# Leaving out the filler products at the front of a retention and feed-forward kernel

## The chip, the cores and the metric

The kernel runs on one core of a Trainium2 chip, as one launch. The metric is the device time of that launch in microseconds (us). Three timed runs of the kernel before gave 626.86, 627.22 and 627.27 us; the median is 627.22 us.

## The reference

Three stages follow each other. The first is a retention with a decay for each head, over 2 batches, 8 heads, 768 positions and 64 elements of a head:

```
for t in range(S):
    state = gamma * state + outer(k[:, :, t], v[:, :, t])
    y[:, :, t] = scale * (q[:, :, t] @ state)          # scale = 1/sqrt(64)
x = y as 1536 rows of 512
g = softplus(x @ w_in);  x = g @ w_out                  # 512 -> 2048 -> 512
xn = x / sqrt(mean(x*x) + 1e-6) * rms_g
out = (silu(xn @ w_gate) * (xn @ w_val)) @ w_out2       # 512 -> 1536 -> 512
```

The weights of the two feed-forward stages arrive as 64-bit floats. They are converted on the chip into a high and a low part, and each of their products is computed as three products of parts.

## The kernel before, in words

**Tiles and stages.** The 1536 rows are 12 chunks of 128 (6 for each batch), and 3 blocks of 512. For each chunk the retention is computed in its chunked form: `step_t` transposes q and k of a chunk on TensorE (`turn`, line 261) and moves them out, q by VectorE (line 263, multiplied by a table of decays) and k by ScalarE (line 268). `step_s` multiplies the two (line 280; two heads at a time, in two PSUM banks), and VectorE multiplies the result by a mask (line 282, one instruction for each bank). `step_y` adds the product with the running state (line 316, not in a batch's first chunk) to the product of the masked scores with v (line 323). `step_u` makes the new state (line 293). Ahead of that, GpSimd multiplies v by decays in `prep` (line 250).

**Order of the work.** Every engine works its instructions off in the order in which the code writes them. The program opens with chunk 0: `keep_busy(6)`, the table of decays (`wide` on VectorE, then `table` with four transposes, line 237), the masks, `step_t(0, 1, (0, 1))`, two more `keep_busy` products, `step_s(0)` and `step_t(1)`. The loop over the first four chunks then runs, for each g, `step_y(g)`, `step_u(g)`, `step_s(g + 1)` and `step_t(g + 2)`. From chunk 4 on, products of the first feed-forward layer (line 340, 512 columns each) stand between the steps of the chunks; after chunk 11 TensorE has feed-forward products alone.

**The fillers.** `keep_busy(n)` takes one PSUM bank and writes n products of a 128 by 128 tile of ones with itself to it (line 214). Nobody reads them. There are ten: six ahead of the table's transposes, one each ahead of the transposes of q and of k of chunk 0, and two ahead of the scores of chunk 0.

**Loads.** q, k and v come by DMA in rows of 64 floats. The queues of SyncE and ScalarE share the halves of q and k of chunk 0; everything after that is issued by SyncE in the order of the code. q, k and v of all chunks share ten buffers (`s2_p`), so the load of v of chunk 2 waits until q of chunk 0 has been transposed.

**Banks.** `bank()` hands out the eight PSUM banks: four from a pool that goes round, and up to four accumulator banks that are lent in between, by a count of the calls (`banks["n"]`). Each `keep_busy` is one such call.

Of the kernel before, what the change touches and what calls it, by code (L numbers as in the profile page):

```python
# [15 lines left out]
P = 128  # L16
# [10 lines left out]
def retention_softplus_swiglu(ctx: ExitStack, tc: tile.TileContext, q, k, v, w_in, w_out,  # L27
                              w_gate, w_val, w_out2, rms_g, decay, out):
    nc = tc.nc
# [30 lines left out]
    def bank(name):  # L60
        n, s = banks["n"], len(banks["spare"])
        banks["n"] += 1
        if (n + 1) * s // (4 + s) > n * s // (4 + s):
            banks["spare"].append(banks["spare"].pop(0))
            return acc_bank(banks["spare"][-1])
        return ps.tile([P, N], F32, tag="ps", name=name)

    def acc_bank(m):
        return pa.tile([P, N], F32, tag=f"acc{m}", name=f"acc{m}")
# [30 lines left out]
    def load_next(g, weight=False):  # L100
        if g + 1 < NCH:
            load(g + 1, 0)
            load(g + 1, 1)
        if weight:
            load_weight()
        if g < NCH:
            load(g, 2)


    ones = const.tile([P, P], F32)  # L110
# [15 lines left out]
    order = []  # L126
# [81 lines left out]
            load_weight()  # L208


    def keep_busy(n):
        t = bank("busy")
        for _ in range(n):
            nc.tensor.matmul(t[:, 0:P], lhsT=ones, rhs=ones, start=True, stop=True)


    x, tr, tp = {}, {}, {}


# [7 lines left out]
    def pair(t, j):  # L227
        return t[:, 2 * j:2 * j + 2, :].rearrange("p h d -> p (h d)")

    def wide():  # L230
        nc.vector.tensor_copy(tab[:, 1].rearrange("p j (e d) -> p j e d", e=2),
                              dec[:, 0, 1, :].rearrange("p (e j) -> p j e", e=2)[:, :, :, None].to_broadcast([P, NP, 2, D]))
# [7 lines left out]
    def masks():  # L240
        nc.vector.scalar_tensor_tensor(out=back, in0=dec[:, 1, 1], scalar=float(D) ** 0.5, in1=dec[:, 0, 0],
                                       op0=ALU.mult, op1=ALU.mult)
        for e in range(2):
            nc.vector.tensor_tensor(out=mask[e], in0=causal[:, None, :].to_broadcast([P, NP, P]),
                                    in1=back.rearrange("p (e j) -> p e j", e=2)[:, e, :, None].to_broadcast([P, NP, P]),
                                    op=ALU.mult)

    def prep(g):
        t = qkv[g][2]
        nc.gpsimd.tensor_tensor(out=t, in0=t, in1=dec[:, 1, 0, :, None].to_broadcast([P, H, D]), op=ALU.mult)  # L250

    def turn(g, busy, order):
        t = at_p.tile([P, 4, NP, P], F32, tag="at", name="at")
        tr[g] = t
        tp[g] = []
        for i in order:
            if busy:
                keep_busy(busy)
            pt = bank("pt").rearrange("p (j t) -> p j t", j=NP)
            for j in range(NP):  # L260
                nc.tensor.transpose(pt[:, j, :], pair(qkv[g][i], j), ident)  # L261
            tp[g].append(pt)
        nc.vector.tensor_tensor(out=t[:, 0], in0=tp[g][order.index(0)], in1=tab[:, 0], op=ALU.mult)
        if g == NCH - 1:
            free.append(WS - 1)

    def turned(g, order):
        nc.scalar.activation(out=tr[g][:, 1], in_=tp.pop(g)[order.index(1)], func=AF.Copy)

    def step_t(g, busy=0, order=(1, 0)):  # L270
        turn(g, busy, order)
        turned(g, order)

    def step_s(g):
        t = tr[g]
        sc = [bank("sc").rearrange("p (j t) -> p j t", j=NP) for _ in range(2)]
        for j in range(NP):
            for e in range(2):
                r = slice(e * D, (e + 1) * D)
                nc.tensor.matmul(sc[e][:, j, :], lhsT=t[r, 1, j, :], rhs=t[r, 0, j, :], start=True, stop=True)  # L280
        for e in range(2):
            nc.vector.tensor_tensor(out=t[:, 2 + e], in0=sc[e], in1=mask[e], op=ALU.mult)
# [252 lines left out]
                step()  # L535

    rg = const.tile([P, KC], F32)
    keep_busy(6)
    wide()
    table()  # L540
    masks()
    step_t(0, 1, (0, 1))
    load_next(1)
    load_weight()
    prep(0)
    keep_busy(2)
    step_s(0)
    step_t(1)
    nc.scalar.activation(out=step, in_=tab[:, 0, :, 0], func=AF.Copy, scale=float(D) ** 0.5)
    for g in range(CB):  # L550
        load_next(g + 2)
        if g:
            load_weight()
        prep(g + 1)
        if g == CB - 1:
            nc.sync.dma_start(out=rg, in_=rms_g.rearrange("(k p) -> p k", p=P))
        step_y(g)
        step_u(g)
        step_s(g + 1)
        flush(False)  # L560
        if g < CB - 1:
            step_t(g + 2)
        flush(False)
        if 0 < g < CB - 1:
            convert()

    pend = None
    for gr in range(NG1):
        for b in range(NB):
# [6 lines left out]
            if gr == 0 and b < NB - 1:  # L576
                for o in range(G1):
                    g = (b + 1) * CB + o
# [27 lines left out]
    for gr in range(NG2):  # L606
        for b in range(NB):
# [8 lines left out]
            n = 0  # L616
# [56 lines left out]
```

## Time and profile before

| | |
|---|---|
| median of the timed runs | 627.22 us (626.86 to 627.27) |
| span of the profiled execution, first to last instruction | 3531.3 us |
| time of the profiled execution around its span | not recorded |
| TensorE busy in it | 3526.4 us (100%), 3308 products |
| VectorE, ScalarE, GpSimd busy | 360.4, 325.9, 187.2 us |
| granted TensorE clock recorded | 1.000 throughout |
| HBM read, written | 45.14 MB, 3.15 MB |

How to read it: the profiled execution took more than five times as long as the timed ones. Its times on TensorE are therefore not those of a timed run, and each reading of it has to say how it is carried over. The page's busy time of an engine counts the stretches in which it works at something; a wait row tells how long an engine stood idle and what ended that.

### The profile page before, as it was taken

To read this page: it belongs to the slowest core of one execution; us is meant where nothing else is said; L and a number is where in the kernel's file an instruction comes from. 1 tells how busy PE (TensorE), PEld (TensorE's weight loads), DVE (VectorE), ACT (ScalarE), POOL (GpSimd) and SP (SyncE) were. 2 spreads that over 40 slices of the span, in tenths; PEclk is the share of its full clock that TensorE was granted. 3 is DMA by queue.
4 is the path that set the end of the run, shared out by engine and by line. 5 is a ranking of instruction groups with operands and counts; after the bars stand their busy time and mean duration, and the time that the engine had idled before them with its cause. 6 is when DMAs were issued, how large, how long until landed. Compare 5 with 4: busy or idle time off the path is not lost.

```text
span 3531.3 us, 8590 instructions
## 1 busy us (share of the span) xinstructions
PE 3526.4 (100%) x3308; PEld 2460.6 (70%) x3308; DVE 360.4 (10%) x613; ACT 325.9 (9%) x555; POOL 187.2 (5%) x156
## 2 busy tenths in 40 slices
PE   9999999999999999999999999999999999999999
PEld 8777666666666666666776766666666666666666
DVE  1111001101101010011111100000110011100000
ACT  0111011111101010011110010000000000000000
POOL 0001000000000000000000000000000000000000
DMA  3110000000000000000000000000000000000000
GB/s 76 45 33 21 6 12 12 18 18 18 12 0 12 18 18 0 6 18 0 6 18 18 6 18 18 0 12 6 18 18 0 12 10 14 0 0 3 9 6 18
DMA packets 65560, 48.84 MB, mean 14 GB/s; under 512 B 39792, under 2 KB 60528, under 8 KB 65520
## 3 DMA queue, kind: packets, MB, share of 16 engines
q1 hardware_dynamic: 64320, 47.90, 4.6%
q8 instruction: 26, 0.43, 0.0%
q10 hardware_dynamic: 1200, 0.39, 0.0%
q14 instruction: 14, 0.11, 0.0%
HBM read 45.14 MB, written 3.15 MB: 14 GB/s over the span
## 4 chain that ended last, share of the span: by engine, by line
PE 100%; DVE 0%; ACT 0%; issue 0%
PE h L340 19%; PE h_w_val L340 14%; PE h_w_gate L340 14%; PE l L376 12%; PE l L494 10%; PE acc L376 9%; PE acc L494 6%; PE acc L340 6%; PE sc L280 1%; PE y L323 1%; PE pt L261 1%; PE acc L261 1%; PE acc L323 1%; PE acc L280 1%; PE acc L293 1%; PE y L316 0%
## 5 line engine op out<-in xcount | busy, mean ns | idle before, releaser
L340 PE MATMUL h<-x,ws_w_in 128*128 128x512 f32 x516 | 699.5, 1697 | 0.0
L340 PEld LDWEIGHTS h<-x,ws_w_in 128*128 128x128 f32 x516 | 469.4, 911 | 209.0 <-issue 209.0
L340 PE MATMUL h_w_val<-xn,ws_w_val 128*128 128x512 f32 x384 | 519.5, 1693 | 0.0
L340 PE MATMUL h_w_gate<-xn,ws_w_gate 128*128 128x512 f32 x372 | 502.9, 1694 | 0.0
L340 PEld LDWEIGHTS h_w_val<-xn,ws_w_val 128*128 128x128 f32 x384 | 351.1, 916 | 156.0 <-issue 156.0
L340 PEld LDWEIGHTS h_w_gate<-xn,ws_w_gate 128*128 128x128 f32 x372 | 340.1, 914 | 151.8 <-issue 151.4
L376 PE MATMUL l<-g,ws_w_out 128*128 128x512 f32 x324 | 438.4, 1691 | 0.0
L376 PEld LDWEIGHTS l<-g,ws_w_out 128*128 128x128 f32 x324 | 295.3, 912 | 131.7 <-issue 129.2
L494 PE MATMUL l<-ws_w_out,g 128*128 128x512 f32 x261 | 354.6, 1697 | 0.0
L376 PE MATMUL acc<-g,ws_w_out 128*128 128x512 f32 x252 | 340.6, 1699 | 0.0
L494 PEld LDWEIGHTS l<-ws_w_out,g 128*128 128x128 f32 x261 | 236.7, 908 | 106.0 <-issue 104.4
L376 PEld LDWEIGHTS acc<-g,ws_w_out 128*128 128x128 f32 x252 | 229.5, 914 | 102.6 <-issue 100.5
L494 PE MATMUL acc<-ws_w_out,g 128*128 128x512 f32 x171 | 231.1, 1696 | 0.0
L494 PEld LDWEIGHTS acc<-ws_w_out,g 128*128 128x128 f32 x171 | 156.4, 915 | 69.9 <-issue 69.1
L171 POOL TENSOR_TENSOR c<-w,c 128x512 uint32<-128x512 uint32 x68 | 86.0, 1264 | 1635.3 <-DVE w L169 1279.8
L360 DVE SCALAR_TENSOR_TENSOR t<-h,t 128x512 f32<-128x512 f32 x43 | 29.7, 692 | 990.7 <-ACT t L359 990.7
L122 ACT ACTIVATE g<-t 128x512 fp32r<-128x512 f32 x84 | 52.9, 630 | 720.5 <-DVE t L475 686.2
L357 ACT ACTIVATE t<-h 128x512 f32<-128x512 f32 x43 | 25.7, 597 | 1002.7 <-PE h L340 1002.7
L471 ACT ACTIVATE t<-t 128x512 f32<-128x512 f32 x36 | 22.7, 630 | 701.1 <-DVE t L470 701.1
L340 PE MATMUL acc<-x,ws_w_in 128*128 128x512 f32 x60 | 82.6, 1715 | 0.0
L340 PE MATMUL acc<-xn,ws_w_gate 128*128 128x512 f32 x60 | 81.9, 1701 | 0.0
L475 DVE TENSOR_TENSOR t<-h_w_val,t 128x512 f32<-128x512 f32 x32 | 22.1, 691 | 559.3 <-PE h_w_val L340 559.3
(128 smaller groups left out, 1579.8 us busy)
## 6 DMA issues: line engine op xcount, KB each, us to landing
st_w_out<-in_moe_w_out_dram SPq DMA_DIRECT2D x28, 512.0 KB, 3.2
st_w_in<-in_moe_w_in_dram SPq DMA_DIRECT2D x16, 512.0 KB, 3.8
st_w_gate<-in_moe_w_gate_dram SPq DMA_DIRECT2D x12, 512.0 KB, 3.5
st_w_val<-in_moe_w_val_dram SPq DMA_DIRECT2D x12, 512.0 KB, 3.5
v<-in_v_dram SPq DMA_DIRECT2D x12, 256.0 KB, 3.8
q<-in_q_dram SPq DMA_DIRECT2D x23, 128.0 KB, 3.5
k<-in_k_dram SPq DMA_DIRECT2D x23, 128.0 KB, 2.6
out_dram<-o SPq DMA_DIRECT2D x11, 256.0 KB, 2.0
```

Source lines behind the costliest of these rows:

```text
L122: nc.scalar.activation(out=hi, in_=src, func=AF.Copy)
L171: nc.gpsimd.tensor_tensor(out=c, in0=w, in1=c, op=ALU.add)
L261: nc.tensor.transpose(pt[:, j, :], pair(qkv[g][i], j), ident)
L280: nc.tensor.matmul(sc[e][:, j, :], lhsT=t[r, 1, j, :], rhs=t[r, 0, j, :], start=True, stop=True)
L293: nc.tensor.matmul(u[e * D:(e + 1) * D, j, :], lhsT=kk[:, h, :], rhs=vv[:, NP * e + j, :], start=True, stop=True, skip_group_check=True)
L323: nc.tensor.matmul(ys[e][h * D:(h + 1) * D, i, :], lhsT=qkv[g][2][:, NP * e + j, :], rhs=t[:, 2 + e, j, :], start=(c == 0 and i == 0), sto ...
L340: nc.tensor.matmul(h, lhsT=w[:, i, kk * P:(kk + 1) * P], rhs=src[:, j, kk, :], start=(n == 0), stop=(n == 3 * KC - 1))
L357: nc.scalar.activation(out=t, in_=h, func=AF.Abs)
L360: nc.vector.scalar_tensor_tensor(out=t, in0=h, scalar=0.0, in1=t, op0=ALU.max, op1=ALU.add)
L376: nc.tensor.matmul(p, lhsT=w[:, i, m * P:(m + 1) * P], rhs=g_t[b, f][:, j, :], start=(n == 0 and f == (0 if keep else fs[0])), stop=(n == ...
L471: nc.scalar.activation(out=t, in_=t, func=AF.Silu)
L494: nc.tensor.matmul(p, lhsT=g_t[b, f][:, j, m * P:(m + 1) * P], rhs=w[:, i, :], start=(n == 0 and f == (0 if keep else grp[0])), stop=(n == ...
```

## The change

All four calls of `keep_busy`, ten products in all, are left out, and the function with them; `turn` and `step_t` lose the argument that asked for it.

```
-    def keep_busy(n):
-        t = bank("busy")
-        for _ in range(n):
-            nc.tensor.matmul(t[:, 0:P], lhsT=ones, rhs=ones, start=True, stop=True)
...
-    def turn(g, busy, order):
+    def turn(g, order):
...
         for i in order:
-            if busy:
-                keep_busy(busy)
             pt = bank("pt").rearrange("p (j t) -> p j t", j=NP)
...
-    keep_busy(6)
     wide()
     table()
     masks()
-    step_t(0, 1, (0, 1))
+    step_t(0, order=(0, 1))
     load_next(1)
     load_weight()
     prep(0)
-    keep_busy(2)
     step_s(0)
```

TensorE's order at the program's start, in the kernel before (`busy` are the fillers, `acc0` to `acc3` lent accumulator banks, `ident` the identity of the transposes, `at` the tile of transposed q and k):

```order
L214 MATMUL busy_130<-ones_109 128x128 [waits DVE_49]
L214 MATMUL busy_130<-ones_109 128x128 x5
L237 MATMUL acc0_138<-ident_111,tab_122 128x128 [waits DVE_49,Pool_49]
L237 MATMUL acc0_138<-ident_111,tab_122 128x128 x3
L214 MATMUL busy_148<-ones_109 128x128
L261 MATMUL acc1_150<-ident_111,q0_95 128x128 [waits DMAHW2_49,DMAHW0_49]
L261 MATMUL acc1_150<-ident_111,q0_95 128x128 x3
L214 MATMUL busy_155<-ones_109 128x128
L261 MATMUL acc2_157<-ident_111,k0_98 128x128 [waits DMAHW4_49,DMAHW3_49]
L261 MATMUL acc2_157<-ident_111,k0_98 128x128 x3
L214 MATMUL busy_175<-ones_109 128x128 x2
```

The same place in the changed kernel, up to the first of the scores:

```order
L231 MATMUL pt_131<-ident_111,tab_122 128x128 [waits DVE_49,Pool_49]
L231 MATMUL pt_131<-ident_111,tab_122 128x128 x3
L253 MATMUL acc0_141<-ident_111,q0_95 128x128 [waits DMAHW2_49,DMAHW0_49]
L253 MATMUL acc0_141<-ident_111,q0_95 128x128 x3
L253 MATMUL pt_146<-ident_111,k0_98 128x128 [waits DMAHW4_49,DMAHW3_49]
L253 MATMUL pt_146<-ident_111,k0_98 128x128 x3
L272 MATMUL acc1_164<-at_140 128x128 [waits DVE_49,Activation_49]
```

The table's transposes are now TensorE's first work, and every transpose follows the one before it with nothing between; the banks shift by the four calls that are gone.

Around chunk 11, where the lent banks change from four to two to none, TensorE's order before (transposes of k and q, the first layer's products, the state's product):

```order
L261 MATMUL pt_1082<-ident_111,k11_907 128x128 [waits DMAHW3_49,DMAHW2_49]
L261 MATMUL pt_1082<-ident_111,k11_907 128x128 x3
L261 MATMUL pt_1087<-ident_111,q11_904 128x128 [waits DMAHW1_49,DMAHW0_49,DVE_49]
L261 MATMUL pt_1087<-ident_111,q11_904 128x128 x3
L340 MATMUL acc2_1094<-x1_533,ws_w_in_589 128x512 [waits PE_49]
L340 MATMUL acc2_1094<-x1_533,ws_w_in_589 128x512 x11
L316 MATMUL y_1119<-at_983,state0_119 64x128 [waits DVE_49]
L316 MATMUL y_1120<-at_983,state0_119 64x128 [waits DVE_49,Activation_49]
```

And in the changed kernel:

```order
L253 MATMUL acc2_1068<-ident_111,k11_893 128x128 [waits DMAHW2_49,DMAHW3_49,DVE_49,PE_49]
L253 MATMUL acc2_1068<-ident_111,k11_893 128x128 x3
L253 MATMUL pt_1073<-ident_111,q11_890 128x128 [waits DMAHW1_49,DMAHW0_49]
L253 MATMUL pt_1073<-ident_111,q11_890 128x128 x3
L332 MATMUL h_1080<-x1_519,ws_w_in_575 128x512 x12
L308 MATMUL acc3_1105<-at_969,state0_119 64x128 [waits DVE_49]
L308 MATMUL y_1106<-at_969,state0_119 64x128
```

The same products stand in the same order; two of the bank waits have moved from q's transposes and the first layer to k's transposes.

## Rows read from the trace of the kernel before

**Rows 1.** The page's head and its busy times by engine.

```profile
span 3531.3 us, 8590 instructions
PE 3526.4 (100%) x3308; PEld 2460.6 (70%) x3308; DVE 360.4 (10%) x613; ACT 325.9 (9%) x555; POOL 187.2 (5%) x156
```

**Rows 2.** Timeline of weight loads: start, duration (us), engine, line, operation.

```profile
1513.84 0.88 PEld L340 LDWEIGHTS h<-x,ws_w_in 128*128 128x128 f32 x1 [0.39 <-issue]
1515.12 0.87 PEld L340 LDWEIGHTS h<-x,ws_w_in 128*128 128x128 f32 x1 [0.40 <-issue]
```

**Rows 3.** Stretches: each engine's busy us, then granted clock, DMA share, GB/s.

```profile
0.00:9.30 9.30, 8.18 (x12) 8.04 (x13) 1.96 (x5) 1.28 (x1) 2.18 (x9) 1.00 0.96 180
9.30:22.70 13.40, 13.40 (x21) 11.22 (x19) 0.69 (x1) 1.19 (x2) 2.08 (x2) 1.00 0.66 133
```

**Rows 4.** The chain that ended last, opening stretch: start, us, engine, tile, line.

```profile
1.12 8.54 PE busy L214 x12
9.65 2.56 PE acc L237 x4
13.67 2.56 PE acc L261 x4
17.50 2.73 PE acc L261 x4
20.24 2.56 PE busy L214 x4
36.54 2.56 PE y L323 x4
39.09 2.73 PE acc L293 x8
118.26 15.87 PE acc L340 x12
```

**Rows 5.** Timeline of the opening on VectorE, ScalarE and TensorE.

```profile
2.84 0.43 DVE L231 COPY tab<-dec 128x512 f32<-128x512 f32 x1 [1.77 <-DMA dec<-decay_dram]
20.27 0.60 ACT L268 ACTIVATE at<-acc 128x512 f32<-128x512 f32 x1 [7.43 <-PE acc L261]
22.72 1.31 PE L280 MATMUL acc<-at 64*128 64x128 f32 x1
26.89 0.98 PE L280 MATMUL acc<-at 64*128 64x128 f32 x1
27.53 0.98 PE L280 MATMUL acc<-at 64*128 64x128 f32 x1
28.54 0.69 DVE L282 TENSOR_TENSOR at<-acc,mask 128x512 f32<-128x512 f32 x1 [11.52 <-PE acc L280]
29.15 0.68 DVE L282 TENSOR_TENSOR at<-sc,mask 128x512 f32<-128x512 f32 x1
```

**Rows 6.** Timeline of the opening: loads on SyncE's queue, GpSimd's work on v.

```profile
1.23 0.42 SPq L83 DMA_DIRECT2D q<-in_q_dram  x1
1.70 0.50 SPq L83 DMA_DIRECT2D k<-in_k_dram  x1
8.01 1.04 POOL L250 TENSOR_TENSOR v<-v,dec 128x512 f32<-128x512 f32 x1 [6.13 <-DMA v<-in_v_dram]
11.76 1.09 SPq L83 DMA_DIRECT2D k<-in_k_dram  x1
12.60 1.04 POOL L250 TENSOR_TENSOR v<-v,dec 128x512 f32<-128x512 f32 x1 [3.55 <-DMA v<-in_v_dram]
16.25 0.37 SPq L80 DMA_DIRECT2D v<-in_v_dram  x1
```

**Rows 7.** Loads of three short windows: tile, queue, count, size, us to landing.

```profile
q<-in_q_dram SPq DMA_DIRECT2D x1, 128.0 KB, 3.4
...
k<-in_k_dram SPq DMA_DIRECT2D x1, 128.0 KB, 3.8
...
k<-in_k_dram SPq DMA_DIRECT2D x1, 128.0 KB, 4.6
```

More of the change, by code (lines that the diff above doesn't have):

```diff
@@ L268, in turned, with step_t @@
         nc.scalar.activation(out=tr[g][:, 1], in_=tp.pop(g)[order.index(1)], func=AF.Copy)
-    def step_t(g, busy=0, order=(1, 0)):
-        turn(g, busy, order)
+    def step_t(g, order=(1, 0)):
+        turn(g, order)
         turned(g, order)
```

## The prediction

> **What bounds the kernel now.** I read the page's head first. TensorE is busy for 3526.4 of 3531.3 us [rows 1]: in the profiled execution nothing else bounds. But that span is 5.63 times the median time, 627.22 us, so the second thing to read is TensorE's pace. In the feed-forward part the weight loads of successive 512-column products start 1.28 us apart [rows 2]. By the loops there are 2448 such products (576 and 576 in the first feed-forward stage, 864 and 432 in the second); at this pace they alone take 3133 us. The timed runs cannot have that pace. The stretches show the clock as 1.00, the upper level of 2.4 GHz, even while that pace holds [rows 3], so the clock column does not explain it. The Trainium skill ("TensorE: Matmul & The Clock Gate", the caveat in "Seeing it yourself") says that clock events in a trace have been seen to be unreliable; this trace agrees, with 1.00 beside 1.28 us.
>
> I carry TensorE's rows over by a factor. It is at least 5.63, if a timed run were all TensorE. I take 6: 3526.4 / 6 = 588 us, which leaves 39 us for launch, waits at the front and the end. A sixth stands for the upper clock, a third for the lower level (1.2 GHz). The other engines and the DMA keep their times; I have no reason to scale them.
>
> Then the opening. In the chain of waits the fillers stand in the path with 8.54 us for the first six and more for the others, behind them the table's transposes, those of q and k (2.56 to 2.73 us for each four), and the scores [rows 4]. Each filler is two records on TensorE (12 for six), 20 records of 0.64 us, the distance of the last two score products' starts [rows 5].
>
> Last, the loads. DMA is 96% busy up to 9.3 us [rows 3]. The second half of q of chunk 0 is issued at 1.23 and lands 3.4 later, at 4.6; k's at 1.70 + 3.8 = 5.5; GpSimd starts on v of chunk 0 at 8.01 and of chunk 1 at 12.60, each at its landing; k of chunk 3 lands at 11.76 + 4.6 = 16.4 [rows 6, 7]. These times owe nothing to TensorE.
>
> **The change, part by part.** First against the profiled execution's own time, its span (what lies around it was not recorded). Twenty records go, 20 x 0.64 = 12.8 us. Given back: TensorE then waits from 1.1 to 3.3 us for VectorE's copy of the table, which starts at 2.84 and takes 0.43 [rows 5], 2.2 us; and the two fillers ahead of the scores covered ScalarE's move of k, 0.60 [rows 5], which is now open. 12.8 - 2.2 - 0.6 = 10.0 us. The loads of chunk 1 are in by 12.6, ahead of the scores' end at about 18, so nothing else is late: an execution with this pace would come to 3521 us, 0.3% less.
>
> In a timed run most of that vanishes, because the loads do not shrink with the factor. I write both openings out with TensorE at the lower level until its clock rises (record 0.21, four transposes 0.85, scores 8 x 0.21 = 1.7, `y` 1.7, `u` 0.9).
>
> Before: six fillers 1.1 to 3.7, table to 4.5, filler to 4.95, q to 5.8, filler to 6.2, k to 7.1, two fillers to 7.9. ScalarE has k ready at 7.1 + 0.6 + 0.1 = 7.8. Scores from 7.9. TensorE has had no pause since 1.1, and I choose to take the upper level from here on: scores to 8.75, two masks of 0.69 on VectorE [rows 5] to about 10.2, transposes of chunk 1 meanwhile, `y(0)` to 10.75, `u(0)` to 11.2, scores of chunk 1 to 12.05, their masks to about 13.8 (VectorE also has x and the state to write). v of chunk 1 is ready at 12.60 + 1.04 = 13.64 [rows 6]: `y(1)` is pinned by VectorE and the load alike, and ends at 14.6.
>
> After: table 3.3 to 4.15, q from its landing 4.7 to 5.55, k to 6.45, ScalarE to 7.1, scores from 7.15: 0.75 us earlier. At the lower level they end at 8.85 and the masks at 10.3, as before. Transposes of chunk 1 to 10.55, `y(0)` to 12.25. If the clock has risen by then, `u(0)` ends at 12.7, scores of chunk 1 at 13.55, masks at 15.0, `y(1)` at 15.55, some 0.95 us later than before.
>
> What takes that up is the next load. v of chunk 2 was issued at 16.25 in the profile, behind q's transposes [rows 6]; in a timed run it follows directly on k of chunk 3. At the 133 to 180 GB/s of these stretches [rows 3] its 256 KB take 1.5 to 2.0 us, and behind a landing at 16.4 that is 17.9 to 18.4, plus 1.04 for GpSimd: `y(2)` cannot start before about 19. In both versions TensorE has the scores and transposes for it done by 18.2. So the front meets again at chunk 2, and what is left is the bank shift.
>
> That shift moves two waits around chunk 11, from q's transposes and the first layer to k's transposes. The trace of before does not show a bank wait as TensorE's idle time there. Its bound is one eviction on either side, 0.69 us as for a mask [rows 5], below nothing too; I take 0, for the same work stands behind both.
>
> Sum: -0.75 at the scores, +0.75 from the slower scores, +0.95 by `y(1)` and -0.95 at the load of v, 0 for the banks. I add 0.2 for a late rise of the clock: 627.4 us.
>
> **A rule that speaks against this.** The clock column never leaves 1.00 [rows 3], so no row shows a rise here. The Trainium skill ("TensorE: Matmul & The Clock Gate", "What's actually happening") says that the array starts at the lower clock and that activity releases it. By that rule the fillers buy an early rise, and without them the front could stay at the lower level; that is the first rival.
>
> **The rivals.**
>
> *Slower: the clock stays down through the front.* If the clock rises late in the kernel after, every us past about 12.5 costs half a us, since the work runs at half pace and its slack at the load of v of chunk 2 is used up. Slower than 0.2% (1.25 us) it becomes if the rise comes after 15; at 20 it costs 3.75 us (631.0). The far end is no rise before the first 512-column products: from the scores at 22.72 to 118.26 [rows 4, 5] are 95.5 us, a third of it 31.8, so that these start at 39 instead of about 25.5: +13.5, 641 us. For it: no row shows when the clock rises, and after the change TensorE's work begins 2.2 us later and pauses twice, for q and for ScalarE, before the scores. Against it: from 7.15 on TensorE has no pause in the working above, as before it had none from 1.1 on, and that leaves until 15 for the rise.
>
> *Faster: the fillers are on the path and no load is.* If v of chunks 1 and 2 lands earlier in timed runs, or if the clock is at its upper level from the start, the scores' 0.75 us is kept: 626.5. With an eviction's wait saved too (0.69) it is 1.45, 625.8. Against it: DMA is at 96% there.
>
> *The banks alone decide.* The front meets again, and the shifted waits around chunk 11 add or save up to 0.69: 626.5 to 627.9.
>
> **How the numbers follow.** A measurement of this kernel can tell about 0.2%, 1.25 us, from no change. The forecast, hidden by the loads with 626.9 to 628.2, has 0.48; the slower rival 0.28; the faster one 0.16, of which 0.10 passes 0.2%; the banks 0.08. So faster 0.10, same 0.48 + 0.06 + 0.08 = 0.62, slower 0.28. The range runs from 626.2 (below lies most of the 0.10) to 630.5, a rise at about 19 us, above which I leave 0.11.
>
> **What would show it.** In a profile of the changed kernel at the timed runs' pace, the scores of chunk 0 start near 7.2 us, not 7.9; `y(2)` starts right behind GpSimd's work on v of chunk 2, at about 19 us; the first 512-column product starts at the same time as before within 0.5 us. A TensorE that never waits for v in the front, with a granted clock at the lower level past 15 us, proves the forecast wrong, and so does a time outside 626.0 to 628.5. If that profile has the slow pace again, its span should be near 3521 us.

## The result and the profile after

The changed kernel is slower: 631.97 us as the median of four runs (630.83 to 632.28) against 627.25 (626.86 to 627.72) for the kernel before, timed beside it. The ratio is 1.0072, with a 95% interval of 1.0058 to 1.0087. Forecast were 627.4 us in a range of 626.2 to 630.5, with most of the chance on no change. The time lies outside the range.

The profiled execution that stands ahead of the prediction had TensorE at about a sixth of the pace of every other profile of this study, and the cause was not found; so here the kernel before is read from a second profile, whose span is 625.6 us and whose own time is 627.37 (1.8 us lie around the span). The profile of the changed kernel has a span of 630.5 and a time of 632.28 us. These are the heads of the two, before first; they answer to [rows 1].

```profile
span 625.6 us, 8590 instructions
PE 615.0 (98%) x3308; PEld 510.1 (82%) x3308; DVE 387.5 (62%) x613; ACT 322.1 (51%) x555; POOL 193.3 (31%) x156
```

```profile
span 630.5 us, 8550 instructions
PE 616.4 (98%) x3288; PEld 509.9 (81%) x3288; DVE 385.7 (61%) x613; ACT 322.0 (51%) x555; POOL 193.5 (31%) x156
```

The 20 records of the ten fillers are gone (3308 to 3288), and TensorE's busy time has still grown.

**The front came out as forecast: almost nothing of its difference is left.** The timeline of the kernel before (start, duration, engine, line, operation): scores of chunk 0, the transposes behind them, `y` of chunk 1, the transposes of k of chunk 3, GpSimd's work on v of chunk 2, `y` of chunk 2, and the first product of 512 columns.

```profile
7.83 0.37 PE L280 MATMUL acc<-at 64*128 64x128 f32 x1 [0.24 <-ACT at L268]
8.49 0.27 PE L280 MATMUL acc<-at 64*128 64x128 f32 x1
8.61 0.27 PE L280 MATMUL acc<-at 64*128 64x128 f32 x1
8.93 0.66 PE L261 MATMUL acc<-ident,k 128*128 128x128 f32 x4
14.15 0.66 PE L323 MATMUL y<-at,v 128*64 128x128 f32 x8
17.57 0.63 PE L261 MATMUL acc<-ident,k 128*128 128x128 f32 x4 [0.77 <-DMA k<-in_k_dram]
18.63 1.04 POOL L250 TENSOR_TENSOR v<-v,dec 128x512 f32<-128x512 f32 x1 [5.04 <-DMA v<-in_v_dram]
19.72 0.66 PE L323 MATMUL acc<-at,v 128*64 128x128 f32 x8 [0.49 <-POOL v L250]
27.41 3.00 PE L340 MATMUL acc<-x,ws_w_in 128*128 128x512 f32 x12
```

The same places in the changed kernel (its transposes of k of chunk 3 have no wait and are not shown):

```profile
7.28 0.58 PE L272 MATMUL acc<-at 64*128 64x128 f32 x1 [0.69 <-ACT at L260]
8.50 0.42 PE L272 MATMUL acc<-at 64*128 64x128 f32 x1
8.71 0.42 PE L272 MATMUL acc<-at 64*128 64x128 f32 x1
9.28 1.12 PE L253 MATMUL acc<-ident,k 128*128 128x128 f32 x4
15.69 0.66 PE L315 MATMUL y<-at,v 128*64 128x128 f32 x8
18.56 1.04 POOL L244 TENSOR_TENSOR v<-v,dec 128x512 f32<-128x512 f32 x1 [5.08 <-DMA v<-in_v_dram]
19.89 0.66 PE L315 MATMUL acc<-at,v 128*64 128x128 f32 x8
27.56 2.99 PE L332 MATMUL acc<-x,ws_w_in 128*128 128x512 f32 x12
```

The scores start 0.55 us earlier, and their products follow each other every 0.21 us instead of every 0.12. That is the pace of the lower level of the clock without the fillers, and of the upper one with them: the four transposes behind the scores take 1.12 and 0.66 us, and four transposes further on take 1.09 us where the granted clock stands as 0.50 and 0.66 us where it stands as 1.00 (shown below). In the front itself the granted clock stands as 1.00 in both traces, so the level is read there from the pace alone. At `y` of chunk 1 the changed kernel is 1.54 us behind. Then the loads take nearly all of it up: the kernel before waits 0.77 us for k of chunk 3 and 0.49 us for v of chunk 2, and the changed kernel, coming later, waits for neither. At `y` of chunk 2 0.17 us is left, and at the first 512-column product 0.15 us.

**The loss lies at one place, 71 to 80 us.** A table of stretches of 2 us there (each engine's busy us with its count, then granted clock, DMA share, GB/s), before and after; [rows 3] have the same columns.

```profile
70.00:72.00 2.00, 1.85 (x23) 1.76 (x24) 1.75 (x3) 1.17 (x3) 1.82 (x2) 1.00 0.55 153
72.00:74.00 2.00, 2.00 (x12) 1.68 (x10) 2.00 (x7) 1.60 (x3) 0.89 (x1) 1.00 0.31 109
74.00:76.00 2.00, 2.00 (x29) 1.38 (x29) 1.97 (x7) 1.48 (x4) 0.41 (x1) 1.00 0.00 0
76.00:78.00 2.00, 1.84 (x42) 1.70 (x39) 1.87 (x3) 1.11 (x3) 1.18 (x1) 1.00 0.09 18
```

```profile
70.00:72.00 2.00, 0.91 (x16) 0.72 (x14) 1.75 (x3) 1.18 (x3) 1.42 (x2) 1.00 0.82 227
72.00:74.00 2.00, 0.00 (x0) 0.00 (x0) 2.00 (x8) 1.74 (x3) 1.28 (x1) 0.82 0.10 35
74.00:76.00 2.00, 1.90 (x9) 1.93 (x10) 1.97 (x4) 0.60 (x1) 0.00 (x0) 0.50 0.00 0
76.00:78.00 2.00, 2.00 (x7) 1.52 (x6) 0.86 (x2) 0.00 (x0) 1.60 (x2) 0.50 0.16 25
78.00:80.00 2.00, 2.00 (x6) 1.62 (x5) 0.00 (x0) 0.00 (x0) 0.67 (x1) 0.50 0.71 237
80.00:82.00 2.00, 2.00 (x33) 1.37 (x34) 0.00 (x0) 1.18 (x2) 0.00 (x0) 0.97 0.00 0
```

In the changed kernel TensorE does nothing from 70.9 to 74.1, and then works at the lower clock, 1.2 GHz, until about 80. The clock's loss adds up from the column: at a granted clock of 0.50, 2 us hold the work of 1. The four stretches from 74 on lose 1 + 1 + 1 + 0.06, less some 0.05 for the 0.1 us of waiting at their start: 3.0 us of work not done. The 0.36 us that the clock lacks from 72 to 74 cost nothing, because TensorE had no work there. VectorE is full in both kernels from 72 to 76 (2.00 and 1.97 of 2 us); in the changed kernel it then runs out of work (0.86 and 0.00 of 2 us), because TensorE is late.

The timeline of VectorE and TensorE in that place of the changed kernel shows what the wait is for:

```profile
68.73 0.63 PE L285 MATMUL acc<-v,k 128*64 128x64 f32 x16
70.45 1.52 DVE L180 SCALAR_TENSOR_TENSOR a<-a,c 128x512 f32<-128x512 f32 x1 [0.25 <-POOL c L171]
71.89 0.68 DVE L123 TENSOR_TENSOR g<-t,g 128x512 fp32r<-128x512 f32 x1
72.49 0.41 DVE L123 TENSOR_TENSOR x<-acc,x 128x256 fp32r<-128x256 f32 x1
72.83 0.41 DVE L123 TENSOR_TENSOR x<-y,x 128x256 fp32r<-128x256 f32 x1
73.16 0.84 DVE L292 SCALAR_TENSOR_TENSOR state<-state,step,acc 128x64 f32<-128x64 f32 x4
73.92 0.68 DVE L274 TENSOR_TENSOR at<-sc,mask 128x512 f32<-128x512 f32 x1
74.10 1.09 PE L253 MATMUL acc<-ident,k 128*128 128x128 f32 x4 [3.19 <-issue]
```

The transposes of k of chunk 11 start 0.10 us behind the update of the state. In the changed order they were given bank acc2, and by the count in `bank()` the product `u` of chunk 9, which the update reads, lies in acc2. TensorE had written it at about 69.4 (68.73 + 0.63); VectorE comes to it at 73.16, 3.8 us later, behind a weight conversion and the splits of g and of x into their high and low parts. The view names no releaser ("issue"); the program's order does, with a wait for VectorE at these transposes. In the kernel before k of chunk 11 has a bank of the pool that goes round, and starts with no wait:

```profile
71.24 0.66 PE L261 MATMUL pt<-ident,k 128*128 128x128 f32 x4
72.09 2.99 PE L340 MATMUL acc<-x,ws_w_in 128*128 128x512 f32 x12
```

### The profile page after: what moved, and what is told of

The parts are those of the page before. It is cut to its first block, busy times and chain, and to the rows that moved or that the text cites. A ratio compares the mean times of both kernels' runs of the same rounds, so it can differ in the third digit from the quotient of the medians.

```text
span 630.5 us, 8550 instructions
## 1 busy us (share of the span) xinstructions
PE 616.4 (98%) x3288; PEld 509.9 (81%) x3288; DVE 385.7 (61%) x613; ACT 322.0 (51%) x555; POOL 193.5 (31%) x156
## 4 chain that ended last, share of the span: by engine, by line
PE 91%; DVE 5%; ACT 2%; issue 1%; DMA 0%; POOL 0%; SPq 0%; POOLq 0%
PE h L332 19%; PE h_w_val L332 14%; PE h_w_gate L332 13%; PE l L368 12%; PE l L486 9%; PE acc L368 9%; PE acc L486 6%; PE acc L332 5%; DVE at L274 1%; DVE w L169 1%; PE acc L272 1%; PE acc L253 1%; DVE a L180 1%; DVE state L292 1%; DVE x L123 1%
## 5 line engine op out<-in xcount | busy, mean ns | idle before, releaser
L332 PE MATMUL h<-x,ws_w_in 128*128 128x512 f32 x528 | 129.6, 395 | 1.6 <-ACT ws_w_in L122 1.6
L332 PEld LDWEIGHTS h<-x,ws_w_in 128*128 128x128 f32 x528 | 100.3, 191 | 23.0 <-ACT ws_w_in L122 2.1
L332 PE MATMUL h_w_val<-xn,ws_w_val 128*128 128x512 f32 x384 | 92.3, 389 | 0.0
L332 PE MATMUL h_w_gate<-xn,ws_w_gate 128*128 128x512 f32 x372 | 89.3, 389 | 0.0
L332 PEld LDWEIGHTS h_w_val<-xn,ws_w_val 128*128 128x128 f32 x384 | 72.0, 188 | 14.9
L332 PEld LDWEIGHTS h_w_gate<-xn,ws_w_gate 128*128 128x128 f32 x372 | 69.8, 188 | 14.5
L368 PE MATMUL l<-g,ws_w_out 128*128 128x512 f32 x324 | 78.0, 389 | 0.0
L368 PEld LDWEIGHTS l<-g,ws_w_out 128*128 128x128 f32 x324 | 60.7, 188 | 12.6
L486 PE MATMUL l<-ws_w_out,g 128*128 128x512 f32 x261 | 63.0, 390 | 0.0
L368 PE MATMUL acc<-g,ws_w_out 128*128 128x512 f32 x252 | 60.8, 391 | 0.0
```

The source lines that it names most:

```text
L332: nc.tensor.matmul(h, lhsT=w[:, i, kk * P:(kk + 1) * P], rhs=src[:, j, kk, :], start=(n == 0), stop=(n == 3 * KC - 1))
L368: nc.tensor.matmul(p, lhsT=w[:, i, m * P:(m + 1) * P], rhs=g_t[b, f][:, j, :], start=(n == 0 and f == (0 if keep else fs[0])), stop=(n == ...
L486: nc.tensor.matmul(p, lhsT=g_t[b, f][:, j, m * P:(m + 1) * P], rhs=w[:, i, :], start=(n == 0 and f == (0 if keep else grp[0])), stop=(n == ...
```

## The experiments

Two theories stood against each other. The bank theory: the four calls of `keep_busy` also counted as calls for a bank, and without them the lent banks fall to other tiles, one of which waits. The filler theory: the fillers' early clock is the whole difference. Each median is of runs with the kernel before timed beside them on the same chip; the first four stood beside a kernel before of 626.9 us (626.61 to 627.83), the next four beside 626.99 (626.48 to 627.42).

**The kernel before once more** (no edit).

> The kernel before once more, for a profile at the pace of the timed runs. Bank theory (the four lost calls for a bank shift the order in which banks are lent; in the changed kernel the transposes of k of chunk 11 then wait 3.2 us for a bank, and the clock falls for 6.8 us behind that wait): here TensorE has no idle of over 1 us between 60 and 80 us of the span, and the granted clock stays 1.00 there. Filler theory (the fillers raise the clock early, and what they save in the front is the whole difference): the first 512-column product starts some 4 to 5 us earlier than in the changed kernel, and the stretch around chunk 11 looks alike in both.

627.37 us. No wait of over 0.5 us on TensorE between 60 and 80 us, the clock at 1.00 there, and the front as shown above: the first 512-column product 0.15 us earlier than after, not 4 to 5. That speaks for the bank theory.

**The banks kept, the products left out.**

```
     def keep_busy(n):
         t = bank("busy")
-        for _ in range(n):
-            nc.tensor.matmul(t[:, 0:P], lhsT=ones, rhs=ones, start=True, stop=True)
```

> The filler products are left out as in the change, but each of their four calls still takes its bank, so that every later tile has the bank it had before. Bank theory: no wait at the transposes of k of chunk 11, no fall of the clock, 626.0 to 628.0 us. Filler theory: as the changed kernel, 631 to 632.5 us. If both share, something between, and the difference to 627.25 is the fillers' own part.

626.84 us (626.29 to 627.63), ratio to before 1.0001 (0.9992 to 1.0010). Without a single filler product the time is that of before: the fillers themselves do nothing that can be measured in it. In this kernel's trace the transposes of k of chunk 11 start with no wait (at 70.76), and the granted clock stays at 1.00. The filler theory falls.

**The fillers kept, outside the count.**

```
     def keep_busy(n):
-        t = bank("busy")
+        t = acc_bank(3)
```

> The fillers stay where they were, all in one lent bank (acc3) taken outside the count, so that all later banks are those of the changed kernel. Bank theory: the 3.2 us wait and the fall of the clock are there, 630.5 to 632.5 us. Filler theory: as the kernel before, 626.9 to 627.7 us.

631.35 us (629.43 to 632.15), ratio 1.0068 (1.0055 to 1.0081). All ten fillers run and the loss is there in full. Its timeline has the wait at the same transposes, and the clock falls for a shorter stretch, all of it behind the wait (0.18 x 2 + 0.5 x 2 + 0.18 x 2 = 1.7 us of work not done):

```profile
74.68 0.63 PE L261 MATMUL acc<-ident,k 128*128 128x128 f32 x4 [3.18 <-issue]
```

```profile
74.00:76.00 2.00, 1.32 (x9) 1.35 (x10) 2.00 (x7) 0.93 (x2) 0.57 (x1) 0.82 0.00 0
76.00:78.00 2.00, 2.00 (x7) 1.52 (x6) 1.40 (x3) 0.00 (x0) 1.02 (x1) 0.50 0.03 3
78.00:80.00 2.00, 2.00 (x8) 1.40 (x6) 0.00 (x0) 0.00 (x0) 1.26 (x2) 0.82 0.86 249
```

**The wait filled with products.**

```
+                    if g == NCH - 2:
+                        t = acc_bank(0)
+                        for _ in range(13):
+                            nc.tensor.matmul(t[:, 0:P], lhsT=ones, rhs=ones, start=True, stop=True)
                     if g + 1 < NCH and g != 2 * CB:
                         step_t(g + 1)
```

> The changed kernel, with 13 products of ones with themselves put ahead of the transposes of k of chunk 11, in a bank that is free there; they fill some 2.8 of the 3.2 us that TensorE waits. The wait itself stays. If the fall of the clock behind the wait is half of the loss, it stays at 1.00 and the time is 631.97 - 3.4 = 628.6 (628 to 629.5) us. If the fall costs nothing or comes all the same, 631 to 632.5 us.

629.73 us (629.31 to 629.95), ratio 1.0044 (1.0032 to 1.0057). The transposes still start at 74.07, but TensorE is at work until then and the clock stays up:

```profile
70.81 3.17 PE L574 MATMUL acc<-ones 128*128 128x128 f32 x26
74.07 0.63 PE L253 MATMUL acc<-ident,k 128*128 128x128 f32 x4
```

```profile
74.00:76.00 2.00, 1.93 (x13) 1.79 (x14) 1.97 (x4) 0.60 (x1) 0.00 (x0) 1.00 0.00 0
76.00:78.00 2.00, 2.00 (x17) 1.40 (x19) 0.83 (x2) 0.08 (x1) 1.63 (x2) 1.00 0.18 31
```

So the loss has two parts. The wait is worth 629.73 - 626.9 = 2.8 us of its 3.2. The fall of the clock is worth the rest of the 4.7 us, some 2. I had expected 3.4, and the median is above the 628 to 629.5 that I gave: the 3.4 counted the part of the fall that lay inside the wait, and the fall is not equally long in every run, as the kernel run once more shows below.

**One call more, at the place.**

```
+                    if g == NCH - 2:
+                        bank("skipped")
                     if g + 1 < NCH and g != 2 * CB:
                         step_t(g + 1)
```

> The changed kernel, with one call for a bank that nothing is written to, just ahead of the transposes of chunk 11; it takes the lent bank, so that k of chunk 11 gets a bank of the ring. All other banks up to there stay those of the changed kernel. If that one place is the whole loss, 626.5 to 627.7 us, no wait there and no fall of the clock. If the shift costs in other places too, 628 to 631 us.

631.33 us (630.82 to 632.66), ratio 1.0073 (1.0060 to 1.0085). A miss: I had expected the loss to go. The transposes of k do start at 70.95 without a wait, but the next lent bank, acc3, now falls to the first layer's product. It holds the scores of chunk 10, which VectorE's second mask reads last:

```profile
74.63 0.67 DVE L274 TENSOR_TENSOR at<-acc,mask 128x512 f32<-128x512 f32 x1
75.36 1.22 PE L332 MATMUL acc<-x,ws_w_in 128*128 128x512 f32 x2 [3.31 <-DVE at L274]
```

The wait is of the same size in another place. In these two cases it is the lent bank, still waiting for VectorE to come to it, that costs the time, whichever tile asks for it.

**The held bank, in the kernel before.**

```
-            pt = bank("pt").rearrange("p (j t) -> p j t", j=NP)
+            pt = bank("pt")
+            if g == NCH - 1 and i == 1:
+                pt = acc_bank(0)
+            pt = pt.rearrange("p (j t) -> p j t", j=NP)
```

> The kernel before with its fillers and its count; only the transposes of k of chunk 11 go to acc0, the bank that holds the state's product of chunk 9. If waiting for that bank is the cause, TensorE waits some 3.2 us there and the time is 629.5 to 632 us, 2.8 us and more above before. If the cause is the fillers or another bank, 626.9 to 627.8 us.

631.87 us (630.81 to 632.80), ratio 1.0082 (1.0069 to 1.0096). In the kernel before acc0 is the bank that holds `u` of chunk 9. Fillers and count are untouched; this one bank alone makes the loss. Its wait:

```profile
73.90 1.01 PE L264 MATMUL acc<-ident,k 128*128 128x128 f32 x4 [3.18 <-issue]
```

**The count begun at four, in the changed kernel.**

```
-    banks = {"spare": list(range(KC)), "n": 0}
+    banks = {"spare": [2, 3, 0, 1], "n": 4}
```

> The changed kernel, with the count of banks begun at 4 and the lent banks turned by two, as the four lost calls would have left them; no other edit. Bank theory: 626.3 to 627.6 us, as before and as the kernel that kept the empty calls. If the empty calls did something of their own there, 628 us and more.

627.07 us (626.51 to 627.30), ratio 1.0000 (0.9992 to 1.0009). By the count, only the first three tiles (table, q and k of chunk 0) then lie otherwise than before; the lent banks of all later tiles are those of the kernel before. The change without its shift costs and gains nothing.

**The changed kernel once more** (no edit).

> The changed kernel once more, timed beside the others. 630.8 to 632.3 us. If the part of the loss above 2.8 us is the clock's fall, single runs should stand in steps: no fall 629.7, a fall of 3.4 us 631.4 or so, one of 6.8 us 632 or so, each with its mean clock below 1.000 by half the fall's share of the span.

631.79 us (629.47 to 632.14), ratio 1.0069 (1.0055 to 1.0083). The steps are there. Each run has a mean granted clock on record: here 629.47 us goes with 1.000, 631.12 and 631.79 with 0.997, 631.85 and 632.14 with 0.994. Over all 24 runs of the four kernels that have the wait and nothing to fill it (the changed kernel, fillers uncounted, one call more, held bank) the clock sorts the times without overlap:

| mean granted clock | runs | time, us |
|---|---|---|
| 1.000 | 2 | 629.43 and 629.47 |
| 0.996 or 0.997 | 12 | 630.81 to 631.79 |
| 0.994 | 10 | 631.85 to 632.80 |

The kernels without the wait have 0.998 to 1.000. So the two runs at 1.000 show the wait alone, some 2.5 us above the kernel before, as the filled wait did; the short fall adds 1.7 us (medians 631.16 and 629.45) and the long one 2.7 (632.15), beside 1.7 and 3.0 us of work lost in the profiles of fillers uncounted (0.996) and of the changed kernel (0.994). What makes the fall short, long or absent is not shown.

**A free bank, in the changed kernel** (the edit of the held bank, on the changed kernel, where acc0 is free by then).

> The changed kernel, its count of banks untouched; only the transposes of k of chunk 11 go to acc0, which VectorE has read long before (its multiplication of q of chunk 10 ends some 1.5 us ahead of them), not to acc2, which waits for the state's update. If that one bank is the whole loss, no wait of over 1 us on TensorE between 60 and 80 us, no fall of the clock, 626.6 to 628.2 us (a later tile, the product with the state of chunk 10, may still wait up to 0.8 us for acc3, which VectorE's mask reads last). If any bank behind the same queue on VectorE takes the wait over, as in the kernel with one more call, 630.5 to 632 us.

627.09 us (626.71 to 628.09) beside 627.08 (626.59 to 627.79), ratio 1.0001 (0.9992 to 1.0010). The count stays shifted everywhere; only k of chunk 11 has another bank. It starts at once, and a later tile, the product with the state of chunk 10 in acc3, waits 0.6 us:

```profile
71.10 0.66 PE L256 MATMUL acc<-ident,k 128*128 128x128 f32 x4
71.94 3.00 PE L335 MATMUL h<-x,ws_w_in 128*128 128x512 f32 x12
75.50 0.32 PE L311 MATMUL acc<-at,state 64*64 64x128 f32 x1 [0.56 <-DVE at L277]
```

So the whole loss, wait and fall of the clock, comes from this one bank. No version came out faster than the kernel before: three without any filler products match it.

## Why the prediction was wrong, step by step

**The factor of 6** held nearly: TensorE's busy times stand as 3526.4 to 615.0, 5.73. So a timed run holds 615 us of TensorE's work and not 588, and 12 us around it, not 39; the forecast of the difference does not hang on that. On the changed kernel's page the row of the first layer's products (count, busy us, mean ns, idle before) gives 129.6 / 528 = 0.245 us for a product, pipeline ends included, where the first profile's page had 699.5 / 516 = 1.36 for the same group, 5.5 times as much.

```profile
L332 PE MATMUL h<-x,ws_w_in 128*128 128x512 f32 x528 | 129.6, 395 | 1.6 <-ACT ws_w_in L122 1.6
```

**The opening, -0.75 at the scores and +0.75 from slower scores**, was right in kind: the scores start at 7.28 against a forecast of 7.15, and at 7.83 against 7.9, 0.55 us apart, and slower scores more than make up for it (the transposes behind them start at 9.28 against 8.93). **The +0.95 by `y(1)`** came out as 1.54. The working was not the same on both sides: before, it left VectorE 0.4 us for other writes and `y(1)` 0.8 us, after, 0.1 and 0.55; like for like it gives about 1.5. **Hidden by the loads** held in its result: GpSimd's work on v of chunk 2 starts at 18.63 and 18.56, and `y` of chunk 2, forecast at about 19, starts at 19.72 and 19.89. But the load of k of chunk 3 took up more of the difference (0.77 us) than that of v (0.49), and in the changed kernel TensorE no longer waits for v: the slack was just enough. That the 0.15 us left are near the 0.2 that I added is partly luck, since the 0.2 was a lump and not worked out.

**The slower rival, the clock that stays down through the front,** fails: by the pace the clock does rise later, but only the 0.15 us of it arrive. Its far end set out from 25.5 us for the first 512-column product, a figure given without its working; that product starts at 27.41. A slower result was given 0.28, and it came by another way.

**The step that failed** is the price of the bank shift: "Its bound is one eviction on either side, 0.69 us as for a mask [rows 5], below nothing too; I take 0, for the same work stands behind both." The place was right, the transposes of k of chunk 11 with their new waits for VectorE and for the bank. The size was wrong, and the rival "The banks alone decide" carried the same wrong size. The bank here is free only when VectorE has come to its read, so the price is not one read's 0.69 us but VectorE's queue ahead of it, 3.19 us of waiting. I had taken the price from a profile in which TensorE was six times slower and VectorE was far ahead of it; there VectorE is busy 10% of the span, and no such queue showed. At the pace of the timed runs VectorE is busy 62%, and 100% from 72 to 74 us. I scaled TensorE's own durations, but not what a faster TensorE does to the others: engines that had been ahead of it fall behind.

**The second part**, the clock's fall behind an idle TensorE, some 2 us of the loss, was not in the sum at all. I had weighed the clock at the front only. The Trainium skill ("TensorE: Matmul & The Clock Gate", "Why this matters for your kernels") advises against idle gaps between bursts of matmuls, since they bring the clock back down; the traces agree, with 0.50 behind a wait of 3.19 us and 1.00 behind the same wait filled with products. By the mean clocks 22 of the 24 runs agree, and two kept 1.000 through the wait.

## What to carry to other kernels

An edit that removes instructions also removes their allocations: where buffers are handed out by a count, compare which buffer every later tile gets and who still has to read it, and price a changed wait by the reader's queue, not by the read. Products that seem to keep the clock up can be tested apart from their side effects by leaving the calls and dropping the products. And a profile in which one engine is far slower than in the timed runs can hide the queues of the others, as it hid VectorE's here.

## What the runs showed that I had not expected

An idle stretch of TensorE of 3.2 us in a dense part was followed by the clock at 0.50, for a length that differed from run to run: 3.0 us of work lost in the changed kernel's profile, 1.7 in that of the kernel with uncounted fillers, by their slices, and by the mean clocks none in two of 24 runs. The first profile's pace of 1.28 us for 512 columns, with a granted clock of 1.00 on record, stays unexplained.
